# Sigmoid attention and a gated feed-forward layer on one core: bursts of QK units cut differently

## The chip, the cores and the metric

The kernel runs on one core of a Trainium2 chip. The metric is the time on the device in microseconds (us), the median of three runs. TensorE (PE in the profile) does the matrix products, ScalarE (ACT) and VectorE (DVE) work on their results, GpSimd (POOL) and SyncE (SP) mostly issue transfers (DMA).

## The reference: what is computed

For 8 batches, 12 heads, 448 positions and a head size of 64, attention with a sigmoid in place of the softmax; then a feed-forward layer on all 3584 positions, with the heads side by side as 768 features:

```python
scores = scale * np.matmul(q, k.transpose(0, 1, 3, 2)) - np.log(S)   # S = 448
attn = 1.0 / (1.0 + np.exp(-scores))
x = np.matmul(attn, v)                    # then to (3584, 768)
gate = np.maximum(x @ w_gate, 0.0)        # w_gate, w_val: (768, 1536)
val = x @ w_val
out = gate * val @ w_out                  # w_out: (1536, 768)
```

As the sigmoid needs no sum over a row, scores can go piece by piece through ScalarE.

## The kernel before

TensorE's instructions stand in the order in which the program writes them. They come in five kinds of pieces:

- **QK unit**: for 4 heads (a group g of 3 in a batch) and one chunk of 64 keys per 448, four products with a quarter of the array each; two sigmoids on ScalarE follow.
- **PV**: for one group, after its 7 QK units, 28 products with a quarter of the array each; two scalings into xT on VectorE follow.
- **gate/value unit** ("f"): for 128 of the 1536 inner features, six products for the gate and six for the value; a relu (ScalarE, in the first half of batch 0 VectorE) and a product into hT (VectorE) follow.
- **down tile** ("y"): for 128 positions, 12 products 512 wide (ya) and 12 products 256 wide (yb), then the two parts go to SBUF and out.
- **transposes** of q and k: on TensorE in batches 0 and 1, by DMA afterwards.

All of them take their PSUM tiles in turn from a ring: 4 tiles while batch 0 runs (its QK units have two pairs of their own), and 8 tiles after that.

```python
rings = [ctx.enter_context(tc.tile_pool(name="ring0", bufs=4, space=bass.MemoryType.PSUM))]
pairp = first_psum.enter_context(tc.tile_pool(name="pairp", bufs=2, space=bass.MemoryType.PSUM))
# ... after batch 0:
first_psum.close()
rings.insert(0, ctx.enter_context(tc.tile_pool(name="ring1", bufs=4, space=bass.MemoryType.PSUM)))

def qk_unit(b, g, c):
    ps = [bank("qk_ps") for _ in range(2)]
    qk(qkT_tiles[(b, g)], c, 0, NCH, lambda hh: ps[hh][:, 0:S])
    PT = PTp.tile([P, 2, 512], FP16, tag="PT", name="PT")
    for hh in range(2):
        sigmoid(PT[:, hh, 0:S], ps[hh][:, 0:S])
    PT_tiles[(b, g, c)] = PT

def gv(b, q0, qn, f, act_relu):
    # ... g_ps and v_ps: a bank each, six matmuls each
    if act_relu:
        nc.scalar.activation(gate_sb[:, 0:qn], ps[0][:, 0:qn], AF.Relu)
    else:
        # ... the same on VectorE
    nc.vector.tensor_tensor(out=hT_tiles[(g, f)][:, o : o + qn],
        in0=gate_sb[:, 0:qn], in1=ps[1][:, 0:qn], op=AOP.mult)

def down(g, t):
    # ... for ya (columns 0 to 512) and yb (512 to 768): a bank, 12 matmuls
        if m0 == 0:
            nc.vector.tensor_scalar(out=ysb[:, m0:m1], in0=ps[:], ...)
        else:
            nc.scalar.activation(ysb[:, m0:m1], ps[:, 0 : m1 - m0], AF.Copy, scale=OUT_SCALE)
```

In batch 0 the queries are cut into two parts (192 and 256 wide), so there are 6 slots (3 groups, 2 parts), each of four steps of QK units; a table says what follows each step:

```python
after = {
    # ...
    (2, 3): slots[1].pv,
    (3, 1): slots[2].pv,
    (3, 2): lambda: ffn_mix("f"),
    (3, 3): second_queries,          # transposes, f, transposes
    (4, 1): slots[3].pv,
    (4, 3): lambda: ffn_mix("f"),
    (5, 0): lambda: ffn_mix("f"),
    (5, 1): slots[4].pv,
    (5, 3): lambda: ffn_mix("ff"),
}
# ...
slots[5].pv()
```

From batch 1 on, the 21 QK units of a batch are cut into bursts at `cuts`. In some bursts a PV stands behind the second unit (`pv_at`; -1 is the last group of the batch before). After each burst comes its share of the feed-forward layer, as `mix` says:

```python
ffn_mix("fff", [(1, lambda: both(1, 0))])
for b in range(1, B):
    cuts = (0, 3, 6, 9, 13, 17, 21) if b == 1 else (0, 5, 8, 13, 16, 21)
    pv_at = {3: 0, 5: 1} if b == 1 else {0: -1, 2: 0, 4: 1}
    # ... mix and hooks, see the change
    for m in range(len(mix)):
        for i, (g, c) in enumerate(order[cuts[m] : cuts[m + 1]]):
            if i == 2 and m in pv_at:
                # ... pv_finish(b - 1) or pv_group(b, pv_at[m])
            qk_unit(b, g, c)
        if m >= 3 and 1 < b < B - 1:
            dma_transposes(b + 1, m - 3)
        # ... loads for the next batch
        ffn_mix(mix[m], hooks.get(m, ()))
```

In batch 1 a hook of burst 4 transposes the first q and k of batch 2: two copies on VectorE, then the DMA, ahead of the last unit of that mix.

Of the kernel before, what the change touches and what calls it, by code (L numbers as in the profile page):

```python
# [12 lines left out]
AOP = mybir.AluOpType  # L13
# [4 lines left out]
def kernel(  # L18
# [15 lines left out]
    NG = H // 4  # L34
    P = 128
    NCH = S // 64
# [3 lines left out]
    QCUT = 3  # L40
# [5 lines left out]
    OUT_SCALE = 1.0 / (XSCALE * XSCALE)  # L46
# [26 lines left out]
    def bank(name):  # L73
        return next_ring().tile([P, 512], FP32, tag="ring", name=name)

    def bank16(name):
        return next_ring().tile([P, 1024], FP16, tag="ring", name=name)
# [5 lines left out]
    def tiles_of(b):  # L83
        if b not in in_tiles:
            in_tiles[b] = tuple(
                inp.tile([P, NPAIR, NCH * D], FP16, tag=t, name=t) for t in ("k16", "q16", "v16")
            )
        return in_tiles[b]

    def rows_of(src, b):  # L90
        return src[b].rearrange("(x r) (t c) d -> (r t) x (c d)", r=2, c=NCH)

    def load(b, g0, g1, which, c0=0, c1=NCH):
        for nm, t16, src in zip("kq", tiles_of(b), (k, q)):
            if nm in which:
                xs, cs = slice(2 * g0, 2 * g1), slice(c0 * D, c1 * D)
                nc.gpsimd.dma_start(t16[:, xs, cs], rows_of(src, b)[:, xs, cs])  # L97
# [10 lines left out]
    KCUT = 4  # L108
    first32 = []
    for src, c1, eng in ((k, KCUT, nc.sync), (q, QCUT, nc.scalar)):  # L110
        ysb = ysbp.tile([P, DM], FP32, tag="ysb", name="ysb")
# [2 lines left out]
        first32.append(t32)  # L114
    zeros = const.tile([P, S], FP16, name="zeros")
    nc.vector.memset(zeros[:], 0.0)  # L116
    load(0, 0, 1, "k", KCUT)
    ident = const.tile([P, P], FP16, name="ident")
    make_identity(nc, ident[:])
    gate = const.tile([P, 2], FP16, name="gate")  # L120
    for g in range(1, NG):
        load(0, g, g + 1, "k")
# [57 lines left out]
    def qkT_of(b, g):  # L180
        if (b, g) not in qkT_tiles:
            qkT_tiles[(b, g)] = qkTp.tile([P, TW, P], FP16, tag="qkT", name="qkT")
        return qkT_tiles[(b, g)]

    def pe_transposes(b, g, ti, c0=0, c1=NCH):
        t16 = in_tiles[b][ti]
        qkT = qkT_of(b, g)
        trt = bank16("trt")
        for c in range(c0, c1):
            for h in range(2):  # L190
                nc.tensor.transpose(  # L191
                    trt[64 * h : 64 * h + 64, c * P : (c + 1) * P],
                    t16[:, 2 * g + h, c * D : (c + 1) * D],
                    ident[:],
                )
        nc.vector.tensor_copy(  # L196
            qkT[:, ti * NCH + c0 : ti * NCH + c1, :].rearrange("p c x -> p (c x)"),
            trt[:, c0 * P : c1 * P],
        )

    def dma_transposes(b, g):
        k16, q16, _ = in_tiles[b]
        rel = relp.tile([P, TW, P], FP16, tag="rel", name="rel")
        for ti, t16 in enumerate((k16, q16)):
            nc.vector.tensor_copy(
                rel[:, ti * NCH : (ti + 1) * NCH, :].rearrange("p c (h d) -> p h c d", h=2),
                t16[:, 2 * g : 2 * g + 2, :].rearrange("p h (c d) -> p h c d", c=NCH),
            )
        nc.sync.dma_start_transpose(
            qkT_of(b, g)[:], rel[:].rearrange("p c x -> p (c x)")  # L210
        )
# [68 lines left out]
# [8 lines that stand above are left out]
    def pv_group(b, g):  # L288
        pv(b, g, 0, S, [PT_tiles.pop((b, g, c))[:, :, 0:S] for c in range(NCH)])
# [32 lines left out]
    def store(g, t, ysb, m0, m1, engines):  # L322
        for i, eng in enumerate(engines):
            j = 2 * t + i
            b, c = 2 * g + j // NCH, j % NCH
            dst = out[b * S : (b + 1) * S, m0:m1].rearrange("(t c) m -> c t m", c=NCH)[c]
            eng.dma_start(dst, ysb[64 * i : 64 * i + 64, m0:m1])

    def down(g, t):
        last = (g, t) == (B // 2 - 1, 2 * S // P - 1)  # L330
        ysb = ysbp.tile([P, DM], FP32, tag="ysb", name="ysb")
        for nm, m0, m1 in (("ya", 0, 512), ("yb", 512, DM)):
            ps = bank(nm)
            for f in range(NFC):
                nc.tensor.matmul(  # L335
                    ps[:, 0 : m1 - m0],
                    hT_tiles[(g, f)][:, t * P : (t + 1) * P],
                    wo[:, f, m0:m1],
                    start=(f == 0),
                    stop=(f == NFC - 1),  # L340
                )
            if m0 == 0:
                nc.vector.tensor_scalar(  # L343
                    out=ysb[:, m0:m1], in0=ps[:], scalar1=OUT_SCALE, scalar2=None, op0=AOP.mult
                )
                if last:
                    store(g, t, ysb, m0, m1, (nc.sync, nc.sync))
            else:
                nc.scalar.activation(  # L349
                    ysb[:, m0:m1], ps[:, 0 : m1 - m0], AF.Copy, scale=OUT_SCALE  # L350
                )
        if last:
            store(g, t, ysb, 512, DM, (nc.sync, nc.scalar))
        else:
            store(g, t, ysb, 0, DM, (nc.sync, nc.sync))
# [11 lines left out]
    def push_down(g, ts):  # L367
        for t in ts:
            y_queue.append(lambda t=t: down(g, t))

    def ffn_mix(kinds, hooks=()):
        hooks = list(hooks)
        for left in range(len(kinds), -1, -1):
            while hooks and hooks[0][0] >= left:
                hooks.pop(0)[1]()
            if left:
                (gv_queue if kinds[len(kinds) - left] == "f" else y_queue).popleft()()
# [10 lines left out]
    slots = [FirstSlot(g, half) for half in range(2) for g in range(NG)]  # L388
    push_first(0, range(0, 6), False)
    def second_queries():  # L390
        pe_transposes(0, 1, 1, QCUT, NCH)
        ffn_mix("f")
        pe_transposes(0, 2, 1, QCUT, NCH)


    after = {
# [12 lines left out]
        (3, 1): slots[2].pv,  # L409
        (3, 2): lambda: ffn_mix("f"),  # L410
        (3, 3): second_queries,
        (4, 1): slots[3].pv,
        (4, 3): lambda: ffn_mix("f"),
        (5, 0): lambda: ffn_mix("f"),
        (5, 1): slots[4].pv,
        (5, 3): lambda: ffn_mix("ff"),
    }
    for i, slot in enumerate(slots):
        for u in range(4):
# [12 lines left out]
    def pv_finish(b):  # L432
        pv_group(b, NG - 1)
        push_gv(b, 0, S, range(NFC))
        if b % 2:
            push_down(b // 2, range(7))
# [5 lines left out]
    def hold(b, g):  # L442
        nc.gpsimd.tensor_copy(gate[0:1, :], qkT_tiles[(b, g)][0:1, 0, 0:2])

    def both(b, g):
        pe_transposes(b, g, 0)
        pe_transposes(b, g, 1)
# [6 lines left out]

    ffn_mix("fff", [(1, lambda: both(1, 0))])
    for b in range(1, B):
        cuts = (0, 3, 6, 9, 13, 17, 21) if b == 1 else (0, 5, 8, 13, 16, 21)
        pv_at = {3: 0, 5: 1} if b == 1 else {0: -1, 2: 0, 4: 1}
        hooks = {}
        if b == 1:  # L460
            mix = ["f" * n for n in (3, 3, 3, 2, 2, 2)]
            hooks = {
                1: [(1, lambda: both(1, 1))],
                3: [(1, lambda: both(1, 2))],
                4: [(1, lambda: dma_transposes(2, 0))],
                5: [(1, late_loads)],
            }
        elif b == 2:
            mix = ["fff", "fff", "ffy", "fyf", "fyf"]
        elif b % 2:  # L470
            mix = ["fyf", "fyf", "ffff", "fyf", "fyf"]
        else:
            mix = ["fff", "fyf", "fyf", "fff", "fyf"]
        for m in range(len(mix)):
            for i, (g, c) in enumerate(order[cuts[m] : cuts[m + 1]]):
                if i == 2 and m in pv_at:
                    if m == 0:
                        pv_finish(b - 1)
                    else:
                        pv_group(b, pv_at[m])  # L480
# [3 lines that stand above are left out]
            if m == 0 and b > 1:  # L484
                dma_transposes(b, 2)
            if b == 1:
                if m == 0:
                    load(2, 0, 1, "kq")
                    load(2, 1, 2, "kq")
                    load(2, 2, 3, "kq")  # L490
            elif m == 0 and b + 1 < B:
                if b == 2:
                    hold(2, 2)
                load(b + 1, 0, 3, "kq")
                load_v(b + 1)
            ffn_mix(mix[m], hooks.get(m, ()))
# [34 lines left out]
```

## Time and profile before

| | us |
|---|---|
| time, median of 3 runs (lowest, highest) | 432.88 (432.74, 434.04) |
| span in the profile | 431.1 |
| TensorE, matmuls | 423.0 busy |
| ScalarE | 211.2 busy, of it 150.8 sigmoids, 54.8 relus, 10.7 yb |
| VectorE | 130.7 busy, of it 61.2 products into hT, 28.4 xT, 19.4 ya |

In the profile a line such as L222 is the line of the kernel, `qk_ps<-qkT` what is written and read, `x8` how many instructions were merged, and what follows an arrow in brackets ended the idle time before them. A matmul's recorded length is longer than the time to the next matmul's start, as they are pipelined; so starts are compared, not lengths.

### The profile page before, as it was taken

To read this page: it belongs to the slowest core of one execution; us is meant where nothing else is said; L and a number is where in the kernel's file an instruction comes from. 1 tells how busy PE (TensorE), PEld (TensorE's weight loads), DVE (VectorE), ACT (ScalarE), POOL (GpSimd) and SP (SyncE) were. 2 spreads that over 40 slices of the span, in tenths; PEclk is the share of its full clock that TensorE was granted. 3 is DMA by queue.
4 is the path that set the end of the run, shared out by engine and by line. 5 is a ranking of instruction groups with operands and counts; after the bars stand their busy time and mean duration, and the time that the engine had idled before them with its cause. 6 is when DMAs were issued, how large, how long until landed. Compare 5 with 4: busy or idle time off the path is not lost.

```text
span 431.1 us, 8609 instructions
## 1 busy us (share of the span) xinstructions
PE 423.0 (98%) x3668; PEld 235.5 (55%) x3668; DVE 130.7 (30%) x250; ACT 211.2 (49%) x451; POOL 49.5 (11%) x73
## 2 busy tenths in 40 slices
PE   8999999999999999999999999999999999999996
PEld 3677775455555455455555555455555545555563
DVE  2453334323322233222331323322332222222111
ACT  4765886645555555454554545655653545122110
POOL 8543203500120002100030000100000000000000
PEclk9999999999999999999999999999999999999999
DMA  9999928999897134955289033721333101100134
GB/s 150 197 202 203 204 52 120 204 203 204 176 165 144 13 72 84 165 100 81 44 127 196 22 76 67 109 55 38 60 73 71 37 2 38 37 2 1 47 101 110
DMA packets 68790, 43.64 MB, mean 101 GB/s; under 512 B 35600, under 2 KB 65168, under 8 KB 68752
## 3 DMA queue, kind: packets, MB, share of 16 engines
q0 software_dynamic: 30736, 23.37, 36.5%
q1 hardware_dynamic: 37664, 19.47, 22.7%
q8 instruction: 28, 0.46, 0.4%
q10 hardware_dynamic: 352, 0.26, 0.2%
q14 instruction: 10, 0.08, 0.1%
HBM read 47.19 MB, written 11.01 MB: 135 GB/s over the span
## 4 chain that ended last, share of the span: by engine, by line
PE 95%; ACT 2%; DMA 1%; DVE 1%; issue 1%; ACTq 0%
PE g_ps L297 26%; PE v_ps L297 25%; PE ya L335 17%; PE qk_ps L222 10%; PE yb L335 9%; PE pv_ps L240 7%; ACT PT L177 1%; PE trt L191 1%; PE warm_ps L160 1%; DMA qkT<-rel 1%; DVE xT L168 0%; DVE qkT L196 0%; ACT ysb L349 0%; DVE zeros L116 0%; ACTq L177 0%
## 5 line engine op out<-in xcount | busy, mean ns | idle before, releaser
L177 ACT ACTIVATE PT<-qk_ps 128x448 f16<-128x448 f32 (+3 forms) x318 | 150.8, 595 | 35.9 <-PE qk_ps L222 35.7
L297 PE MATMUL g_ps<-xT,wg 128*128 128x448 f16 (+2 forms) x648 | 127.7, 332 | 0.2 <-DVE xT L168 0.2
L297 PE MATMUL v_ps<-xT,wv 128*128 128x448 f16 (+2 forms) x648 | 126.8, 332 | 0.0
L315 DVE TENSOR_TENSOR hT<-gate_sb,v_ps 128x448 f16<-128x448 f32 (+2 forms) x108 | 61.2, 569 | 195.5 <-PE v_ps L297 113.7
L306 ACT ACTIVATE gate_sb<-g_ps 128x448 f32<-128x448 f32 (+2 forms) x102 | 54.8, 545 | 75.6 <-PE g_ps L297 73.5
L335 PEld LDWEIGHTS <-hT 128*128 128x128 f16 x672 | 65.8, 98 | 46.9
L297 PEld LDWEIGHTS <-wv 128*128 128x128 f16 x648 | 62.5, 98 | 47.4 <-issue 0.7
L297 PEld LDWEIGHTS <-wg 128*128 128x128 f16 x648 | 58.8, 98 | 49.4 <-issue 10.8
L335 PE MATMUL ya<-wo,hT 128*128 128x512 f16 x336 | 77.1, 379 | 0.0
L349 ACT ACTIVATE ysb<-yb 128x256 f32<-128x256 f32 x28 | 10.7, 383 | 102.1 <-PE yb L335 102.1
L222 PE MATMUL qk_ps<-qkT 64*64 64x448 f16 (+2 forms) x756 | 51.8, 336 | 1.9 <-ACT PT L177 1.1
L335 PE MATMUL yb<-wo,hT 128*128 128x256 f16 x336 | 41.2, 273 | 0.0
L240 PE MATMUL pv_ps<-PT,v 64*64 64x448 f16 (+2 forms) x756 | 37.5, 329 | 0.7 <-issue 0.6
L168 DVE TENSOR_SCALAR xT<-pv_ps 128x448 f16<-128x448 f32 (+2 forms) x54 | 28.4, 568 | 27.4 <-PE pv_ps L240 27.4
L222 PEld LDWEIGHTS <-qkT 64*64 64x64 f16 x756 | 20.5, 105 | 29.1 <-issue 20.7
L343 DVE TENSOR_SCALAR ysb<-ya 128x512 f32<-128x512 f32 x28 | 19.4, 692 | 55.8 <-PE ya L335 55.8
L240 PEld LDWEIGHTS <-v 64*64 64x64 f16 x756 | 21.6, 107 | 12.4 <-issue 1.8
L101 POOL DMA_DIRECT2D v<-in_v_dram x8 | 6.0, 748 | 175.7 <-PE qk_ps L222 173.2
L97 POOL DMA_DIRECT2D q<-in_q_dram x15 | 11.4, 758 | 11.9 <-DVE xT L168 6.0
L97 POOL DMA_DIRECT2D k<-in_k_dram x14 | 10.9, 776 | 5.9 <-DMA wv<-in_moe_w_val_dram 1.9
L103 POOL DMA_DIRECT2D v<-in_v_dram x16 | 10.1, 634 | 2.7 <-DMA wv<-in_moe_w_val_dram 2.1
L196 DVE COPY qkT<-trt 128x896 f16<-128x896 f16 (+2 forms) x16 | 7.6, 504 | 7.0 <-PE trt L191 7.0
(24 smaller groups left out, 53.1 us busy)
## 6 DMA issues: line engine op xcount, KB each, us to landing
out_dram<-ysb SPq DMA_DIRECT2D x54, 192.0 KB, 2.7
k<-in_k_dram POOLq DMA_DIRECT2D x5, 672.0 KB, 15.0
q<-in_q_dram POOLq DMA_DIRECT2D x5, 672.0 KB, 17.5
v<-in_v_dram POOLq DMA_DIRECT2D x8, 336.0 KB, 4.9
v<-in_v_dram POOLq DMA_DIRECT2D x16, 168.0 KB, 5.8
k<-in_k_dram POOLq DMA_DIRECT2D x8, 224.0 KB, 10.4
wo<-in_moe_w_out_dram POOLq DMA_DIRECT2D x1, 1536.0 KB, 12.2
q<-in_q_dram POOLq DMA_DIRECT2D x6, 224.0 KB, 12.1
```

The source lines that it names most:

```text
L97: nc.gpsimd.dma_start(t16[:, xs, cs], rows_of(src, b)[:, xs, cs])
L103: nc.gpsimd.dma_start(v16[64 - 64 * r : P - 64 * r, 1::2, :], rows_of(v, b)[64 * r : 64 * r + 64, 1::2, :])
L168: nc.vector.tensor_scalar(out=xT_of(b, pr)[:, q0 : q0 + qn], in0=src, scalar1=XSCALE, scalar2=None, op0=AOP.mult,)
L177: nc.scalar.activation(PT_ap, ps_ap, AF.Sigmoid, bias=sig_bias, scale=qk_scale)
L222: nc.tensor.matmul(out_of(hh)[o : o + 64, :], qkT[rows, c, cols], qkT[rows, NCH + c0 : NCH + c1, cols], start=True, stop=True, tile_positi ...
L240: nc.tensor.matmul(ps[hh][64 * r : 64 * r + 64, 0:qn], v16[rows, 2 * g + hh, c * D : (c + 1) * D], pieces[c][rows, hh, :], start=(c == 0), ...
L297: nc.tensor.matmul(ps[-1][:, 0:qn], wt[:, dc, f * P : (f + 1) * P], xT_tiles[(b, dc)][:, q0 : q0 + qn], start=(dc == 0), stop=(dc == NDC - 1),
L306: nc.scalar.activation(gate_sb[:, 0:qn], ps[0][:, 0:qn], AF.Relu)
L315: nc.vector.tensor_tensor(out=hT_tiles[(g, f)][:, o : o + qn], in0=gate_sb[:, 0:qn], in1=ps[1][:, 0:qn], op=AOP.mult,)
L335: nc.tensor.matmul(ps[:, 0 : m1 - m0], hT_tiles[(g, f)][:, t * P : (t + 1) * P], wo[:, f, m0:m1], start=(f == 0), stop=(f == NFC - 1),)
L343: nc.vector.tensor_scalar(out=ysb[:, m0:m1], in0=ps[:], scalar1=OUT_SCALE, scalar2=None, op0=AOP.mult)
L349: nc.scalar.activation(ysb[:, m0:m1], ps[:, 0 : m1 - m0], AF.Copy, scale=OUT_SCALE)
```

## The change

It does not add or remove a product. It moves pieces on TensorE, and it moves the emptying of yb (all but the last tile's) from ScalarE to VectorE.

- From batch 2 on, the bursts are 4, 4, 4, 4, 5 units instead of 5, 3, 5, 3, 5; those with PV are still the first, third and fifth. The down tile stands at the end of a mix instead of in its middle, so that it comes just before the next burst, and VectorE empties it, for ScalarE to be free for the sigmoids.
- In batch 0 the transposes of the second queries stand together, one gate/value unit goes between the last two steps of slot 4, and the two units ahead of the last PV go to batch 1, whose mixes become 3, 3, 3, 3, 3, 2 units instead of 3, 3, 3, 2, 2, 2.
- At the start the identity matrix for the transposes is made before a load is issued, not after it.

```diff
-    load(0, 0, 1, "k", KCUT)
     ident = const.tile([P, P], FP16, name="ident")
     make_identity(nc, ident[:])
+    load(0, 0, 1, "k", KCUT)
@@
-            if m0 == 0:
+            if m0 == 0 or not last:
                 nc.vector.tensor_scalar(
-                    out=ysb[:, m0:m1], in0=ps[:], scalar1=OUT_SCALE, scalar2=None, op0=AOP.mult
+                    out=ysb[:, m0:m1], in0=ps[:, 0 : m1 - m0], scalar1=OUT_SCALE, scalar2=None, op0=AOP.mult
                 )
@@
     def second_queries():
-        pe_transposes(0, 1, 1, QCUT, NCH)
-        ffn_mix("f")
-        pe_transposes(0, 2, 1, QCUT, NCH)
+        for g in range(1, NG):
+            pe_transposes(0, g, 1, QCUT, NCH)
@@
         (4, 1): slots[3].pv,
+        (4, 2): lambda: ffn_mix("f"),
         (4, 3): lambda: ffn_mix("f"),
         (5, 0): lambda: ffn_mix("f"),
         (5, 1): slots[4].pv,
-        (5, 3): lambda: ffn_mix("ff"),
     }
@@
-        cuts = (0, 3, 6, 9, 13, 17, 21) if b == 1 else (0, 5, 8, 13, 16, 21)
+        cuts = (0, 3, 6, 9, 13, 17, 21) if b == 1 else (0, 4, 8, 12, 16, 21)
@@
-            mix = ["f" * n for n in (3, 3, 3, 2, 2, 2)]
+            mix = ["f" * n for n in (3, 3, 3, 3, 3, 2)]
@@
         elif b == 2:
-            mix = ["fff", "fff", "ffy", "fyf", "fyf"]
+            mix = ["fff", "fff", "ffy", "ffy", "ffy"]
         elif b % 2:
-            mix = ["fyf", "fyf", "ffff", "fyf", "fyf"]
+            mix = ["ffy", "ffy", "ffy", "fff", "fffy"]
         else:
-            mix = ["fff", "fyf", "fyf", "fff", "fyf"]
+            mix = ["ffy", "fff", "ffy", "fff", "ffy"]
```

## The prediction

> **What bounds the kernel now.** I read the page first (engine shares), then TensorE's timeline stretch by stretch, then ScalarE's timeline and the chain of waits where TensorE's blocks were too long. The page says that TensorE is the kernel:
>
> ```profile
> PE 423.0 (98%) x3668; PEld 235.5 (55%) x3668; DVE 130.7 (30%) x250; ACT 211.2 (49%) x451; POOL 49.5 (11%) x73
> ```
>
> The granted clock is full in every slice after the start, so only time in which TensorE does not stream can be won. A busy TensorE can still hide such time, so I compare start to start. Six matmuls of 448 columns (one g or v block) take 1.14 us from start to start where nothing disturbs them, 0.189 us each. The four quarter-array matmuls of one QK unit run side by side and also take 0.189 us when undisturbed, and the 28 of a PV take 7 x 0.189 = 1.32 us. Against these I hold the timeline of TensorE (start, length with overlap, operation), here a burst of 5 QK units with PV inside and a burst of 3 without:
>
> ```profile
> 186.41 0.57 PE L222 MATMUL qk_ps<-qkT 64*64 64x448 f16 x8
> 186.82 1.49 PE L240 MATMUL pv_ps<-PT,v 64*64 64x448 f16 x28
> 188.14 0.98 PE L222 MATMUL qk_ps<-qkT 64*64 64x448 f16 x12
> 189.06 1.31 PE L297 MATMUL g_ps<-xT,wg 128*128 128x448 f16 x6
> ...
> 197.60 0.76 PE L222 MATMUL qk_ps<-qkT 64*64 64x448 f16 x12
> 198.29 1.31 PE L297 MATMUL g_ps<-xT,wg 128*128 128x448 f16 x6
> ```
>
> With PV the burst lasts 189.06 - 186.41 = 2.65 us, where 5 x 0.189 + 1.32 = 2.27 are work: 0.38 over. Without PV it lasts 0.69, where 0.57 are work: 0.12 over. The v block ahead of each takes 1.23 instead of 1.14, so entering a burst costs 0.09 and leaving it about 0.10. What the PV burst has beyond that is 0.25 us, all in its last three units (188.14 to 189.06 is 0.92 for 0.57 of work).
>
> Batch 1 holds the shapes that the change introduces everywhere, a PV burst of 4 (50.78) and a burst of 4 without PV (56.72), and then one that goes wrong (59.82):
>
> ```profile
> 50.78 0.57 PE L222 MATMUL qk_ps<-qkT 64*64 64x448 f16 x8
> 51.19 1.49 PE L240 MATMUL pv_ps<-PT,v 64*64 64x448 f16 x28
> 52.51 0.55 PE L222 MATMUL qk_ps<-qkT 64*64 64x448 f16 x8
> 52.99 0.83 PE L297 MATMUL g_ps<-xT,wg 128*128 128x256 f16 x6
> ...
> 56.72 1.03 PE L222 MATMUL qk_ps<-qkT 64*64 64x448 f16 x16
> 57.75 0.66 PE L297 MATMUL g_ps<-xT,wg 128*128 128x192 f16 x6
> ...
> 59.82 1.36 PE L222 MATMUL qk_ps<-qkT 64*64 64x448 f16 x8
> ...
> 63.23 0.83 PE L297 MATMUL g_ps<-xT,wg 128*128 128x256 f16 x6
> ```
>
> They last 2.21, 1.03 and 3.41 us, for 2.08, 0.76 and 2.08 of work: 0.13, 0.27 and 1.33 over. ScalarE's timeline says what the third waits for, and the chain of waits what follows it:
>
> ```profile
> 57.15 3.60 ACT L177 ACTIVATE PT<-qk_ps 128x448 f16<-128x448 f32 x8 [0.59 <-PE qk_ps L222]
> ```
> ```profile
> 62.06 4.07 DMA qkT<-rel
> ```
>
> Eight sigmoids take 3.60 us and the next burst starts 3.1 us after the last. In batch 0 (timeline again) two QK units wait for a sigmoid, starts 0.92 and 0.60 us after the block before:
>
> ```profile
> 23.90 0.30 PE L222 MATMUL qk_ps<-qkT 64*64 64x256 f16 x4 [0.50 <-ACT PT L177]
> ...
> 28.27 0.30 PE L222 MATMUL qk_ps<-qkT 64*64 64x256 f16 x4 [0.20 <-ACT PT L177]
> ```
>
> **What the Trainium skill says.** "TensorEngine Tiling (Array Packing)", section Tiling Modes, says that changing the tiling mode drains TensorE; the trace agrees, about 0.09 us at each of the two borders of a burst. So the number of bursts is a cost of its own, and after batch 1 the change keeps it at five per batch. "Perfetto Trace Analysis", section Identifying the Most-Contended Engine, reads a gap that repeats on the saturated engine as a sign of too little PSUM for the next tile; the 0.25 us in every PV burst of 5 is such a gap. "Runtime: NRT & Kernel Launch", section Instruction fetch mechanics, says that instructions come in blocks of 256; the page's instruction queue q8 has 28 packets of 0.46 MB, which fits TensorE's 7338 instructions, and I take the two stalls by "issue" in batch 0 (0.72 us at 16.20, 0.22 at 22.40) for that.
>
> **Bursts after batch 1.** After batch 0 the kernel has a ring of 8 PSUM tiles; a QK unit takes 2, a PV 2, a gate/value unit 2, a down tile 2. A PV burst of 5 takes 12, so its fifth unit writes where its second one did, and waits for the fourth sigmoid. The first sigmoid starts 0.43 us into the burst, they follow each other by 0.42, one lasts 0.55: the fourth ends at 0.43 + 3 x 0.42 + 0.55 = 2.24. The fifth unit could have started at 0.40 + 1.32 + 0.38 = 2.10. That and the step to the next tile are the 0.25. A PV burst of 4 takes 10 tiles and nothing in it waits: batch 1 shows 0.13 over instead of 0.38. The new cuts (0, 4, 8, 12, 16, 21) make two of the three PV bursts of a batch bursts of 4; the last keeps 5. In batches 2 to 7 that is 12 bursts x 0.25 = 3.0 us removed.
>
> The units taken away go to the bursts without PV, 3 to 4. These take all 8 tiles, so the g block behind them waits for the first sigmoid: 0.43 + 0.54 + 0.05 = 1.02 into the burst, where it could start at 0.88. The burst at 56.72 shows it: 1.03 against 0.69 for three, less one unit's 0.19 is 0.14, of which the g block gives back 0.01. 12 x 0.13 = 1.6 us added. A down tile ahead of such a burst, emptied by VectorE, frees the last two tiles in time: 256 columns take about 0.42 us (the 128x256 scaling of xT on VectorE takes 0.42), begin at 0.10, end near 0.52, and the fourth unit asks at 0.59. On ScalarE it took 0.38, from 0.11 to 0.49, so this move gains nothing by itself; 27 operations leave ScalarE, which is 49% busy, and 27 reach VectorE, at 30%. Only batch 2 puts such a burst behind a gate/value unit, whose product (0.62 us) frees its tile near 0.8: 0.1 added. Together 3.0 - 1.6 - 0.1 = 1.3 us gained.
>
> **Batch 1.** Two gate/value units move here from batch 0, one to each of the two bursts at the end. The burst at 59.82 waits now because eight sigmoids, two relus and two products have to pass in 3.1 us. With three units ahead of it the start moves to 1.02 + 1.31 + 0.99 + 0.99 + 0.09 = 4.4 us after the burst before, and the sigmoids are done at about 4.0. I leave 0.2 of the 1.2 us beyond a smooth burst, for the first product and the PV's tiles: 1.0 gained. Behind it batch 2 waits 0.22 us for its transposed q and k, sent at 62.06 and landed 4.07 later. The copies that feed this transfer stand behind the second product, so they move with the sigmoids; I work out 5.65 + 4.1 = 9.75 us from the burst of 4, against 9.55 for TensorE. The same 0.2 stays.
>
> **Batch 0.** A unit moved between the last two QK units of slot 4 covers the wait at 23.90 (0.66 over). Two transposes side by side save two borders, 0.19. But with one unit less ahead, the q copies are not ready when slot 4 wants them (about 0.4 lost), the instruction block of 22.40 comes no earlier (some 0.5 more), and the last PV no longer has two units (2.0 us) between it and its sigmoids: it waits about 1.0 us, of which the 0.36 at 31.48 for xT come back. ScalarE paces this stretch either way. I count 0.1 us gained. Making the identity first delays a piece of k by 0.5 us; it landed at 5.63 and is used at 6.72, so 0.
>
> **Sum.** 1.3 + 1.0 + 0.1 = 2.4 us: 432.88 - 2.4 = 430.5 us.
>
> **Rivals.** (1) The units put into bursts without PV cost as much as the others gain: then the 12 x 0.13 would be 12 x 0.25, and with the rest the time is 431.9. The one such burst in the trace speaks against it, but it is narrow evidence. (2) The gain of batch 1 is lost to the transposes that batch 2 waits for, should these be held by the arrival of batch 2's q and k instead of by VectorE's order: 431.5. Against it: they landed by 52.2, nine us before they are copied. (3) The 4-unit bursts behind a down tile run with no wait, as the author may hope: then 1.6 is not paid and the time is 428.9. Against it: the wait is for the first sigmoid, which neither the down tile nor VectorE brings forward. (4) ScalarE's relief or VectorE's new load moves the bound: VectorE would go from 30% to 33%, so neither.
>
> **Range and chances.** The terms are small and mostly read from bursts of the same shape; batch 0 may be off by 0.5 us either way, batch 1 by 0.4, the bursts by 0.6. 8 times in 10 it should lie between 429.3 and 431.8 us. 2% would be 8.7 us, more than all the waits that the change touches, so 0.01 for faster, 0.985 for within, 0.005 for slower.
>
> **What would show it.** In the changed profile: PV bursts of 4 of 2.2 us and bursts of 4 without PV of 1.02 to 1.03 us in batches 2 to 7; the last PV burst of a batch still at 2.65; batch 1's last PV burst near 2.4 instead of 3.41; batch 2's first QK near 65 instead of 66.17; batch 1's first QK near 34.1 instead of 36.87 (two units of 1.31 us fewer ahead of it, and the 0.1). Wrong would be: a new wait of bursts for ya or yb, a later landing of the transposes, or bursts without PV well over 1.03.

## The result, and the profile after

Six runs of the changed kernel have a median of 431.66 us (431.17 to 432.34), six of the kernel before on the same chip 432.94 us (432.74 to 434.04). The ratio is 0.9968 with a 95% interval of [0.9955, 0.9982]: about 1.3 us faster. The prediction was 430.5 us. The time lies within its range and within 2%, but the gain is little more than half of the 2.4 us predicted.

From the profile's page of the changed kernel, the engine shares (busy us, share of the span, count) and the group of the yb operations that moved (columns: busy us, mean ns of one, idle time ahead of them):

```profile
PE 419.6 (98%) x3668; PEld 236.0 (55%) x3668; DVE 141.8 (33%) x277; ACT 201.1 (47%) x424; POOL 49.4 (11%) x73
...
L343 DVE TENSOR_SCALAR ysb<-yb 128x256 f32<-128x256 f32 x27 | 11.5, 425 | 16.7 <-PE yb L335 16.7
```

TensorE still has 98%, and the 27 operations are now VectorE's. The page says no more than that. Where the time went is read from start to start on TensorE, between four points that both kernels have:

| stretch on TensorE | before | after | gained |
|---|---|---|---|
| start to batch 1's first QK unit | 36.87 | 34.15, and 2.62 for the two units moved out | 0.10 |
| batch 1: to batch 2's first QK unit | 29.30 | 31.88, less 2.62 for the two units moved in | 0.04 |
| batches 2 to 7: to the start of the last yb block | 359.38 | 358.08 | 1.30 |
| from there to the end of the span | 5.49 | 5.42 | 0.07 |
| span | 431.05 | 429.53 | 1.52 |

(2.62 us is two units of 256 columns at 1.31 us each. The last stretch holds only the last yb block and its way out, which the change leaves alone; its 0.07 is scatter.) The prediction had 0.1, 1.0, 1.3 and nothing for the four stretches. So nearly the whole difference is in batch 1.

**Batches 2 to 7.** TensorE's timeline of the changed kernel, in order: a burst of 4 behind a down tile, a PV burst of 4, and the one PV burst of 5 of a batch (columns: start, length with overlap, operation).

```profile
177.90 0.96 PE L222 MATMUL qk_ps<-qkT 64*64 64x448 f16 x16
178.92 1.30 PE L297 MATMUL g_ps<-xT,wg 128*128 128x448 f16 x6
...
185.82 0.57 PE L222 MATMUL qk_ps<-qkT 64*64 64x448 f16 x8
186.22 1.49 PE L240 MATMUL pv_ps<-PT,v 64*64 64x448 f16 x28
187.55 0.55 PE L222 MATMUL qk_ps<-qkT 64*64 64x448 f16 x8
188.03 1.31 PE L297 MATMUL g_ps<-xT,wg 128*128 128x448 f16 x6
...
204.49 0.57 PE L222 MATMUL qk_ps<-qkT 64*64 64x448 f16 x8
204.89 1.49 PE L240 MATMUL pv_ps<-PT,v 64*64 64x448 f16 x28
206.22 0.98 PE L222 MATMUL qk_ps<-qkT 64*64 64x448 f16 x12
207.13 1.31 PE L297 MATMUL g_ps<-xT,wg 128*128 128x448 f16 x6
```

They last 1.02, 2.21 and 2.64 us. Counted over the six batches there are 12 PV bursts of 4 at 2.21, six of 5 at 2.64, and 12 bursts of 4 without PV: eleven at 1.02 and one, in batch 2 behind a gate/value unit, at 1.16:

```profile
75.15 1.23 PE L222 MATMUL qk_ps<-qkT 64*64 64x448 f16 x16
76.31 1.31 PE L297 MATMUL g_ps<-xT,wg 128*128 128x448 f16 x6
```

**Batch 1.** Its last PV burst, which lasted 3.41 us before, is nearly smooth now (TensorE's timeline of the changed kernel, with the start of batch 2 at its end):

```profile
60.57 0.57 PE L222 MATMUL qk_ps<-qkT 64*64 64x448 f16 x8
60.98 1.77 PE L240 MATMUL pv_ps<-PT,v 64*64 64x448 f16 x28
...
63.06 0.83 PE L297 MATMUL g_ps<-xT,wg 128*128 128x256 f16 x6
...
66.03 0.57 PE L222 MATMUL qk_ps<-qkT 64*64 64x448 f16 x8 [0.18 <-DMA qkT<-rel]
```

63.06 - 60.57 is 2.49 us: 0.93 gained. But the first PV burst of the batch, 2.21 us before, has a wait that was not there (same view):

```profile
48.70 0.57 PE L222 MATMUL qk_ps<-qkT 64*64 64x448 f16 x8
49.11 0.46 PE L240 MATMUL pv_ps<-PT,v 64*64 64x448 f16 x3
49.94 1.51 PE L240 MATMUL pv_ps<-PT,v 64*64 64x448 f16 x25 [0.37 <-DMA v<-in_v_dram]
...
51.76 0.67 PE L297 MATMUL g_ps<-xT,wg 128*128 128x192 f16 x6
```

It lasts 51.76 - 48.70 = 3.06 us, 0.85 more than before. Three matmuls run, then the PV stands until v is there, and goes on at 49.94. The chain of waits of the changed kernel has it (columns: start, length, what):

```profile
37.30 12.60 DMA v<-in_v_dram
49.90 0.04 issue
```

0.93 gained and 0.85 given back leave nearly nothing of batch 1.

### The profile page after: what moved, and what is told of

It reads as the page before. It is cut to its first block, busy times and chain, and to the rows that moved or that the text cites. A ratio compares the mean times of both kernels' runs of the same rounds, so it can differ in the third digit from the quotient of the medians.

```text
span 429.5 us, 8581 instructions
## 1 busy us (share of the span) xinstructions
PE 419.6 (98%) x3668; PEld 236.0 (55%) x3668; DVE 141.8 (33%) x277; ACT 201.1 (47%) x424; POOL 49.4 (11%) x73
## 4 chain that ended last, share of the span: by engine, by line
PE 85%; DMA 10%; POOL 2%; ACT 1%; issue 0%; DVE 0%; POOLq 0%
PE g_ps L297 24%; PE v_ps L297 23%; PE ya L335 17%; PE yb L335 9%; PE pv_ps L240 6%; PE qk_ps L222 6%; DMA k<-in_k_dram 3%; DMA v<-in_v_dram 3%; DMA wg<-in_moe_w_gate_dram 3%; ACT PT L177 1%; DMA qkT<-rel 1%; POOL q L97 1%; POOL k L97 1%; POOL v L103 0%; DVE xT L168 0%
## 5 line engine op out<-in xcount | busy, mean ns | idle before, releaser
L297 PEld LDWEIGHTS <-wg 128*128 128x128 f16 x648 | 59.7, 98 | 52.9 <-issue 10.8
L222 PE MATMUL qk_ps<-qkT 64*64 64x448 f16 (+2 forms) x756 | 48.9, 336 | 1.9 <-ACT PT L177 0.8
L343 DVE TENSOR_SCALAR ysb<-yb 128x256 f32<-128x256 f32 x27 | 11.5, 425 | 16.7 <-PE yb L335 16.7
L349 ACT ACTIVATE ysb<-yb 128x256 f32<-128x256 f32 x1 | 0.4, 384 | 27.9 <-PE yb L335 27.9
```

The source lines that it names most:

```text
L222: nc.tensor.matmul(out_of(hh)[o : o + 64, :], qkT[rows, c, cols], qkT[rows, NCH + c0 : NCH + c1, cols], start=True, stop=True, tile_positi ...
L297: nc.tensor.matmul(ps[-1][:, 0:qn], wt[:, dc, f * P : (f + 1) * P], xT_tiles[(b, dc)][:, q0 : q0 + qn], start=(dc == 0), stop=(dc == NDC - 1),
L343: nc.vector.tensor_scalar(out=ysb[:, m0:m1], in0=ps[:, 0 : m1 - m0], scalar1=OUT_SCALE, scalar2=None, op0=AOP.mult)
```

## The experiments

Two theories stand against each other for the missing gain. **T1:** the two units that left batch 0 bring batch 1's first PV 2.08 us earlier on TensorE (51.19 to 49.11), while its v lands when it did (the last two of its three parts, before: 49.12 and 49.99 us, after: 49.15 and 49.90). So the PV now meets the transfer. **T2:** the early part (the changes up to batch 1) is worth nothing for another reason: batch 2 waits for its transposed q and k anyway (0.25 us over at 66.03), and what is gained ahead of that is lost there. For the late batches the questions were whether the yb move matters, whether the down tile's place does, and what the fifth unit of a PV burst waits for.

### v sent earlier

```diff
-    load(1, 2, 3, "kq")
     load_v(1)
+    load(1, 2, 3, "kq")
```

> The changed kernel with batch 1's v sent before the q and k of its third group, not after them. Theory (the gain of batch 1 was lost to the arrival of v): the first PV of batch 1 runs in 1.32 us instead of 2.00, its burst lasts 2.2 us instead of 3.06, and the time is about 0.85 us under the changed kernel's, near 430.8. Rival (the burst is held by ScalarE's backlog or by instruction fetch): the burst stays near 3.06 and the time at 431.7.

430.96 us against 433.33 for before on that chip, ratio 0.9952 [0.9939, 0.9965]. TensorE's timeline of this run:

```profile
48.78 0.57 PE L222 MATMUL qk_ps<-qkT 64*64 64x448 f16 x8
49.18 1.49 PE L240 MATMUL pv_ps<-PT,v 64*64 64x448 f16 x28
...
50.98 0.67 PE L297 MATMUL g_ps<-xT,wg 128*128 128x192 f16 x6
```

The burst is back at 2.20 us, and batch 2's first QK unit starts at 65.25 instead of 66.03. The 0.78 us came through to batch 2, although batch 2 goes on waiting for its transposes (0.17 us of idle time there): these moved forward with everything else. So T1 holds, and T2 falls as the reason for the loss.

### The late part alone, the early part alone

The late part alone is the kernel before with the new cuts, the new mixes from batch 2 on, and yb on VectorE:

```diff
-            if m0 == 0:
+            if m0 == 0 or not last:
-        cuts = (0, 3, 6, 9, 13, 17, 21) if b == 1 else (0, 5, 8, 13, 16, 21)
+        cuts = (0, 3, 6, 9, 13, 17, 21) if b == 1 else (0, 4, 8, 12, 16, 21)
-            mix = ["fff", "fff", "ffy", "fyf", "fyf"]
+            mix = ["fff", "fff", "ffy", "ffy", "ffy"]
-            mix = ["fyf", "fyf", "ffff", "fyf", "fyf"]
+            mix = ["ffy", "ffy", "ffy", "fff", "fffy"]
-            mix = ["fff", "fyf", "fyf", "fff", "fyf"]
+            mix = ["ffy", "fff", "ffy", "fff", "ffy"]
```

> The kernel before with only the part from batch 2 on (cuts, mixes, yb on VectorE). Theory: all of the net gain is there, about 1.3 us, near 431.6. Rival (the gain comes from batches 0 and 1): near 432.9.

432.23 us against 433.33, ratio 0.9978 [0.9968, 0.9987], or 0.6 to 1.4 us. From batch 2's first QK unit to the last yb block it takes 358.09 us, the changed kernel 358.08. Batch 1's last PV burst is the old one, 3.41 us.

The early part alone is the changed kernel with those lines put back:

```diff
-            if m0 == 0 or not last:
+            if m0 == 0:
-        cuts = (0, 3, 6, 9, 13, 17, 21) if b == 1 else (0, 4, 8, 12, 16, 21)
+        cuts = (0, 3, 6, 9, 13, 17, 21) if b == 1 else (0, 5, 8, 13, 16, 21)
     # the mixes of b >= 2 likewise
```

> The changed kernel with the part from batch 2 on undone (old cuts and mixes, yb on ScalarE); batches 0 and 1 and the start are as changed. Theory: 0.1 to 0.2 us under the kernel before, near 432.8: batch 1's last PV burst is 0.9 shorter and its first 0.9 longer. Rival (the early part is worth the 1.1 us that I had predicted, and the rest is worth nothing): near 431.8.

433.05 us against 433.33, ratio 0.9995 [0.9987, 1.0003]: it can't be told from nothing. TensorE's timeline shows both halves of it again: batch 1's first PV burst stops for v and lasts 51.68 - 48.52 = 3.16 us, its last lasts 2.50. So the measured gain of the change is that of its late part, and its early part earns only when v comes sooner: with v first the ratio, 0.9952 [0.9939, 0.9965], lies below the whole interval of the late part alone on the same chip.

### yb emptied by ScalarE again

```diff
-            if m0 == 0 or not last:
+            if m0 == 0:
```

> The changed kernel with yb emptied by ScalarE again. Theory (the first sigmoid of a burst waits for its QK unit, not for ScalarE): bursts of 4 without PV stay at 1.02 us and the time at 431.7 within 0.2. Rival (ScalarE has to be free for the sigmoids, as the change has it): bursts of 4 grow by 0.1 to 0.3 us, 11 of them by 1 to 3 us in all, 432.7 to 434.7.

431.83 us against 433.33, ratio 0.9967 [0.9956, 0.9979], the same ratio as the change. The burst of 4 behind a down tile, in this run's timeline of TensorE and of ScalarE:

```profile
178.11 0.95 PE L222 MATMUL qk_ps<-qkT 64*64 64x448 f16 x16
179.13 1.30 PE L297 MATMUL g_ps<-xT,wg 128*128 128x448 f16 x6
```
```profile
178.22 0.38 ACT L349 ACTIVATE ysb<-yb 128x256 f32<-128x256 f32 x1 [4.49 <-PE yb L335]
178.54 3.60 ACT L177 ACTIVATE PT<-qk_ps 128x448 f16<-128x448 f32 x8
```

The burst still lasts 1.02 us. On ScalarE the copy takes 0.38 us and begins when yb is ready, and the first sigmoid follows it at 0.43 after the burst's start, when its scores are there anyway (in the changed kernel, where ScalarE is free, the first sigmoid starts at 178.32, which is 0.42 into the burst at 177.90). The move to VectorE has no effect on the time that these runs show.

### The down tile in the middle of its mix

```diff
-            mix = ["fff", "fff", "ffy", "ffy", "ffy"]
+            mix = ["fff", "fff", "fyf", "fyf", "fyf"]
-            mix = ["ffy", "ffy", "ffy", "fff", "fffy"]
+            mix = ["fyf", "fyf", "fyf", "fff", "ffyf"]
-            mix = ["ffy", "fff", "ffy", "fff", "ffy"]
+            mix = ["fyf", "fff", "fyf", "fff", "fyf"]
```

> The changed kernel with the down tile back in the middle of its mix, so that 11 more bursts of 4 without PV stand behind a gate/value unit (yb stays on VectorE). Theory (such a burst waits for the tile of the last product, which the changed kernel shows once, 1.16 us at 75.15 instead of 1.02): 11 x 0.14 = 1.5 us more than the changed kernel, near 433.2. Rival (the order inside a mix is free): 431.7.

434.53 us against 433.24, ratio 1.0025 [1.0014, 1.0036]: slower than the kernel before. All 12 bursts of 4 without PV are as the one in batch 2 now, and the batches from 2 on take 360.43 us, 2.35 more than the changed kernel. TensorE's timeline of this run:

```profile
90.90 1.49 PE L335 MATMUL yb<-wo,hT 128*128 128x256 f16 x12 [0.46 <-DMA wo<-in_moe_w_out_dram]
...
126.22 1.23 PE L222 MATMUL qk_ps<-qkT 64*64 64x448 f16 x16
127.39 1.31 PE L297 MATMUL g_ps<-xT,wg 128*128 128x448 f16 x6
```

In such a burst the fourth unit waits for the tile of the last product: three of its four products start 0.85 us into the burst instead of 0.60, as VectorE ends that product at 0.80. A burst of 1.17 us instead of 1.02, with the block behind it, is 0.155 us lost; eleven of them make 1.7. The rest was in neither expectation: the first down tile stands one unit earlier, and its yb meets the second part of the output weights, which is still on its way (0.62 us over). 1.7 + 0.6 is the 2.35. So the place of the down tile is what makes bursts of 4 pay. Without it the new cuts lose: 360.43 us against 359.38 before, and still 359.8 without the 0.62.

### Half of the sigmoids left out

Every second sigmoid from batch 1 on is left out; VectorE scales these scores instead, so the output is not the reference's. With ScalarE's stretch half as long, a PV burst of 5 should have no wait for the fourth sigmoid.

```diff
-        for hh in range(2):
-            sigmoid(PT[:, hh, 0:S], ps[hh][:, 0:S])
+        sigmoid(PT[:, 0, 0:S], ps[0][:, 0:S])
+        nc.vector.tensor_scalar(
+            out=PT[:, 1, 0:S], in0=ps[1][:, 0:S], scalar1=qk_scale, scalar2=None, op0=AOP.mult
+        )
```

> The changed kernel with every second sigmoid from batch 1 on left out: VectorE scales these scores into PT in its place. ScalarE so reaches the second QK unit's tiles earlier. Theory (a PV burst of 5 waits 0.25 us for the fourth sigmoid): the last PV burst of batches 2 to 7 falls from 2.65 to 2.40 us, 6 x 0.25 = 1.5 us, and the bursts of 4 without PV stay at 1.02, as the g block behind them needs the first sigmoid, which is still there: near 430.2, perhaps 0.2 less by batch 1. Rival (the 0.25 is a cost of going from PV to QK, not a wait): 2.65 stays, 431.7.

431.74 us against 433.24, ratio 0.9964 [0.995, 0.9978]; against the changed kernel's 0.9968 that shows no gain. Five of the six PV bursts of 5 fell from 2.64 only to 2.61, and one rose to 2.81, as VectorE was still busy with scores there and began to scale xT 2.15 us into the burst instead of 1.93. Timeline of TensorE, then the chain of waits, for one of them:

```profile
152.68 0.57 PE L222 MATMUL qk_ps<-qkT 64*64 64x448 f16 x8
153.08 1.49 PE L240 MATMUL pv_ps<-PT,v 64*64 64x448 f16 x28
154.41 0.74 PE L222 MATMUL qk_ps<-qkT 64*64 64x448 f16 x12
155.29 1.29 PE L299 MATMUL g_ps<-xT,wg 128*128 128x448 f16 x6
```
```profile
153.25 1.38 PE pv_ps L240 x27
154.63 0.62 DVE xT L168
155.25 0.04 issue
155.29 1.29 PE g_ps L299 x6
```

The three last units now run as one piece of 0.74 us instead of 0.98: the fifth no longer waits for a sigmoid. But the g block behind it starts as late as before, because it waits for the first of the two scalings of the PV into xT. The ring says why. The burst takes 12 tiles, 1 to 4 for two units, 5 and 6 for the PV, 7 and 8, then 1 to 4 again. The g block takes the next one, 5, which is the PV's first and is free when VectorE has scaled it. VectorE's added work did not make this wait: in the changed kernel, too, that scaling ends 2.56 us into each PV burst of 5. A burst of 4 ends two tiles sooner, so its g block takes tile 3, which the third sigmoid empties at 1.84, well ahead of the block's start at 2.21. So a PV burst of 5 has two waits that end within 0.03 us of each other, and only the shorter burst removes both.

The last PV burst of batch 1 has no wait at all in this run: 2.21 us, against 2.49 in the changed kernel. The first still waits for v (2.86 us).

### A version that beats both: three more moves

To the earlier v, the next kernel adds that batch 2's first transposing transfer starts right behind batch 1's burst of 4, two units sooner (the hook's number counts the units that follow it in the mix, itself included):

```diff
-    load(1, 2, 3, "kq")
     load_v(1)
+    load(1, 2, 3, "kq")
@@
-                4: [(1, lambda: dma_transposes(2, 0))],
+                4: [(3, lambda: dma_transposes(2, 0))],
```

> As the run with batch 1's v first, and the transfer that transposes batch 2's first q and k is started right behind batch 1's burst of 4, ahead of its three gate/value units instead of ahead of the last one. Theory (this transfer stands behind two products, not behind the arrival of q and k): it starts about 4 us earlier, the wait of 0.25 us ahead of batch 2 goes, near 430.7. Rival (the arrival of q and k holds it): the wait stays, 430.96.

430.39 us against 433.24, ratio 0.9936 [0.9921, 0.9951]. Batch 1's last PV burst and batch 2's first QK unit are 5.22 us apart (60.15 and 65.37), in the changed kernel and with v first alone 5.46 (60.57 and 66.03 in the first): the wait for the transposes is gone. The transfer starts at 57.05 instead of 61.10 with v first alone, the 4 us of the theory.

Then, in the last batch, the last PV goes ahead of its mix's down tile instead of behind it, so that the gate/value units that read its xT find it scaled:

```diff
-            ffn_mix(mix[m], hooks.get(m, ()))
-    pv_finish(B - 1)
+            if b == B - 1 and m == len(mix) - 1:
+                ffn_mix("fff")
+                pv_finish(B - 1)
+                ffn_mix("y")
+            else:
+                ffn_mix(mix[m], hooks.get(m, ()))
```

> As the run before it in this list, and in batch 7 the last down tile of batch pair 2 goes behind the last PV instead of ahead of it. Theory: the down tile covers the two scalings of xT that the first gate block waits 0.36 us for, and nothing else changes: near 430.3. Rival (the wait only moves to another tile): 430.7.

430.09 us against 433.24, ratio 0.9927 [0.9912, 0.9942]. The two times are too close for their intervals to part them, but the traces do: from batch 2 to the last yb block it takes 357.73 us, 0.35 less than the changed kernel. That kernel's timeline at this place, and this one's:

```profile
369.07 1.52 PE L240 MATMUL pv_ps<-PT,v 64*64 64x448 f16 x28
370.52 1.13 PE L297 MATMUL g_ps<-xT,wg 128*128 128x448 f16 x5
371.83 0.35 PE L297 MATMUL g_ps<-xT,wg 128*128 128x448 f16 x1 [0.18 <-DVE xT L168]
```
```profile
363.76 1.52 PE L240 MATMUL pv_ps<-PT,v 64*64 64x448 f16 x28
365.22 2.76 PE L335 MATMUL ya<-wo,hT 128*128 128x512 f16 x12
```

The last of six g matmuls started 371.83 - 370.52 = 1.31 us after the first, where five steps of 0.189 make 0.95. With 3.9 us of the down tile between, nothing waits.

The changed kernel, run once more beside the last version:

> The changed kernel itself once more, beside the next run on the same chip: 431.7 within 0.4 if the chips agree; a shift of more than that would have to be taken off the other comparisons.

431.94 us against 433.21, ratio 0.9963 [0.9949, 0.9976], as the first time; its first PV burst of batch 1 takes 3.50 us in this trace. Last, batch 0 in another order. The queries of the second part are sent ahead of the first weights and transposed one step earlier, the first two PVs come one step later, and the gate/value units stand where slots 4 and 5 wait:

```diff
-    load_gv(0, 2)
     load(0, 1, NG, "q", QCUT)
+    load_gv(0, 2)
@@
-        (2, 2): slots[0].pv,
-        (2, 3): slots[1].pv,
+        (2, 3): slots[0].pv,
+        (3, 0): slots[1].pv,
         (3, 1): slots[2].pv,
-        (3, 2): lambda: ffn_mix("f"),
-        (3, 3): second_queries,
+        (3, 2): second_queries,
+        (4, 0): lambda: ffn_mix("f"),
         (4, 1): slots[3].pv,
         (4, 2): lambda: ffn_mix("f"),
-        (4, 3): lambda: ffn_mix("f"),
         (5, 0): lambda: ffn_mix("f"),
         (5, 1): slots[4].pv,
+        (5, 2): lambda: ffn_mix("f"),
     }
```

> The fastest version so far, and batch 0 ordered so that ScalarE does not run dry: the second queries are sent ahead of the first weights and transposed right after step (3, 2), the first two PVs stand one step later, and the four gate/value units stand behind (4, 0), (4, 2), (5, 0) and (5, 2), each time with a QK unit issued ahead of them. Theory (ScalarE paces batch 0 from slot 3 on, and its idle stretches of 0.9 and 0.8 us ahead of slots 4 and 5 are the rest of what can be won there): the first QK of batch 1 moves from near 34.0 to near 32.9, the time from 430.1 to about 429.0. Rival (weights or queries then arrive too late, or instruction fetch paces it): 430.1 or more.

429.14 us (428.96 to 429.71) against 433.21 for the kernel before and 431.94 for the changed one, all on the same chip; the ratio to before is 0.9906 [0.9893, 0.992]. All four runs lie under every run of the changed kernel. Batch 1's first QK unit starts at 33.47, against 34.15. The expected 32.9 was not reached. On the way TensorE waits for value weights, which are sent later now (0.28 us idle at 20.03), and stands for 0.60 us at 22.13 (last section). The time came near the expected 429.0 all the same, but the trace accounts for only 0.38 us of it (33.85 to 33.47), and the interval overlaps that of the version without this step: what the new order of batch 0 gains is not shown.

## Why the prediction was right and wrong

**Bursts after batch 1 (1.3 us): right, and by its steps.** PV bursts of 4 take 2.21 us (2.2 predicted), bursts of 4 behind a down tile 1.02 (1.02 to 1.03), the last PV burst of a batch stays at 2.64. The stretch gained 1.30, with the late part alone 1.29. The burst behind a gate/value unit costs 0.14 more than the others, 0.1 predicted.

**The reason given for the 0.25 us was half of it.** The prediction has the fifth unit wait for the fourth sigmoid, and its sum explains 2.24 - 2.10 = 0.14 us and a step of no stated size. In the burst at 204.49 that wait is there: the sigmoid ends at 2.28, and three of the fifth unit's four products start at 2.33 instead of 2.11. With half of the sigmoids gone it is gone too, but the burst keeps 2.61 of its 2.64 us: the g block behind it now waits for the PV's scaling. Two tiles fewer remove the one wait and the other, so the size was right with half of the reason. What the prediction takes from the Trainium skill, "Perfetto Trace Analysis", stands in its section Optimization Strategy and says that a gap that repeats on the engine that should be saturated can mean too little SBUF or PSUM for the next tile; here both waits are for PSUM tiles.

**yb on VectorE gains nothing by itself: right.** The ratio without it is 0.9967, with it 0.9968. The reasoning was that ScalarE frees yb's tile at 0.49 us into the burst and the fourth unit asks at 0.59; the burst of 1.02 us with yb on ScalarE agrees. What the change needs is only the place of the down tile (1.7 us of bursts without it).

**Batch 1 (1.0 us): this is the step that failed.** "I leave 0.2 of the 1.2 us beyond a smooth burst ...: 1.0 gained" was right for that one burst: 3.41 fell to 2.49, 0.93 gained, and the run with half the sigmoids shows that the other 0.28 is ScalarE's. What was missing is the burst at the other end of the batch. The prediction moved two units from ahead of batch 1 into its last bursts, and wrote that its first QK would start at 34.1, 2.7 us earlier. (The first PV burst came 2.08 us earlier, at 48.70 instead of 50.78: units come from a queue, and wider ones stand ahead of it now.) It did not ask which transfers batch 1 was just in time for. v was: landed at 49.99 us, used from 51.19. With the PV at 49.11 that slack of 1.2 us is used up, and the wait is 0.85. The stream that brings v did not move with TensorE: in all eight traces of kernels that send v last it lands between 49.46 and 50.59 us, whether its PV is due at 49 us or at 51 to 52. In the six of them that have the two units moved, the burst takes 2.69 to 3.50 us, so the loss is 0.5 to 1.3 us, and the 0.85 is what the trace above has. Between 30 and 56 us the loads ran at a mean of 197 GB/s before and 198 after; the last two parts of v in that stretch (KB each, us from issue to landing), before and after:

```profile
v<-in_v_dram POOLq DMA_DIRECT2D x2, 168.0 KB, 12.5
```
```profile
v<-in_v_dram POOLq DMA_DIRECT2D x2, 168.0 KB, 12.8
```

Rival (2) of the prediction had the right kind of loss, a transfer that batch 1's gain runs into, and put it at 431.5 us, close to what was measured. But it named batch 2's q and k, and the run with v sent first shows that these let the gain through; that its number came so near was luck.

**Batch 2 behind it (0.2 us of wait): right.** 0.25 us over at 66.03, the transfer sent at 61.88 and landed 4.10 later. The start near 65 was missed by the wait for v; with v first it is 65.25.

**Batch 0 (0.1 us): a gain of 0.2 in its later part, the rest left open.** The first QK unit of batch 1 came at 34.15, that is 0.10 gained. But in nine traces that share the changed batch 0 it lies between 33.85 and 34.59, so this number alone can't show a term of 0.1. What scatters is the landing of the second queries: their transposes start 0.04 to 0.05 us after it in all nine (TensorE's timeline, before and after):

```profile
19.60 0.41 PE L191 MATMUL trt<-ident,q 128*64 128x128 f16 x8
```
```profile
19.70 0.64 PE L191 MATMUL trt<-ident,q 128*64 128x128 f16 x16 [0.17 <-DMA q<-in_q_dram]
```

From these transposes to batch 1 it takes 17.27 us in both traces with the old batch 0, and 14.45 + 2.62 = 17.07 in six of the nine: 0.20 gained. Of the term's parts, the wait at 23.90 for a sigmoid is gone, as said, and the last PV of batch 0 now waits for its sigmoids, as said:

```profile
23.68 0.30 PE L222 MATMUL qk_ps<-qkT 64*64 64x256 f16 x4
23.91 0.67 PE L297 MATMUL g_ps<-xT,wg 128*128 128x192 f16 x6
...
29.02 0.79 PE L240 MATMUL pv_ps<-PT,v 64*64 64x256 f16 x12 [0.24 <-ACT PT L177]
```

The 0.5 us that the prediction lost to an instruction block near 22.40 are not in this trace; three of the nine have 0.26 to 0.53 us there, which is why they are over 14.45. Whether making the identity first costs or gains was not tried by itself.

**The range** of 429.3 to 431.8 held the time only just. It gave batch 1 an error of 0.4 us, where 0.85 was lost to one wait.

## What to carry to other kernels

When work is moved from ahead of a stage to behind it, everything that the stage reads comes due earlier by the length of that work: list each transfer of the stage with its landing and its first use, and see whether the slack is longer than the move. In a ring of PSUM tiles, count the tiles of a burst against the ring and look at both ends of the overrun, the tiles that the last units take and the one that the next block takes; a shorter burst frees both at once. What stands in front of a burst counts by the time its tiles come free, too: a gate/value unit there cost 0.14 us more than a down tile.

## What the runs showed of the hardware

Two things were not expected. TensorE stands at single places of batch 0 without any wait that the profile shows. From its timeline, in the last version and in the kernel before:

```profile
20.87 0.82 PE L240 MATMUL pv_ps<-PT,v 64*64 64x256 f16 x23
22.13 0.38 PE L240 MATMUL pv_ps<-PT,v 64*64 64x256 f16 x5 [0.44 <-issue]
```
```profile
14.98 0.66 PE L240 MATMUL pv_ps<-PT,v 64*64 64x192 f16 x23
16.20 0.32 PE L240 MATMUL pv_ps<-PT,v 64*64 64x192 f16 x5 [0.56 <-issue]
```

0.60 us over in the first, 0.72 in the second, both in the middle of a PV. The Trainium skill, "Runtime: NRT & Kernel Launch", section Instruction fetch mechanics, calls the cost of a new instruction block mostly hidden; the prediction took the stalls for the fetch of such a block, and the twelve traces speak for it. From 9 us on they have ten idle times of 0.1 us or more put down to "issue". All ten stand ahead of the 224th or the 352nd matmul, which are 128 matmuls or, with their weight loads, 256 instructions apart. All ten of these matmuls start 1.30 to 1.67 us after the end of a 16 KB packet on the instruction queue q8 (13.37 to 14.54 us for the stall at 16.20), and in no trace does the 224th or the 352nd start sooner after it. Where something else holds TensorE longer, as v of batch 0 does in the changed kernel (the 224th at 16.06, 2.38 us after the packet), there is no stall. None comes after 22.2 us. No run changed the fetch, so this is close evidence and not a test. (The page has 2 x 3668 = 7336 instructions of TensorE, the prediction 7338.)

The start of the program, up to batch 1, scatters by 0.7 us between traces with the same batch 0, where the batches from 2 on repeat to 0.02 us (358.08 to 358.10 in six traces of kernels with the same bursts there). Most of the scatter is the landing of the second queries, 19.28 to 20.09 us. So a term in batches 2 to 7 can be read from a single trace, and one in batch 0 only from such a landing on.
